# Decode layers on one core: split V load of head 5, two heads summed by columns, a last norm with both sums in one product

## The chip, the cores and the metric

The kernel runs on one core of a Trainium2 chip. The metric is the device time of one execution in microseconds (us). Three executions of the kernel before the change took 175.13, 175.47 and 176.53 us, median 175.47. One more execution was taken by the hardware profiler.

## What is computed

Four rows x of 512 elements (a batch of 4, one position each) go through attention, a gated MLP, the same attention and the same MLP, each with a residual. All inputs are bf16, and both layers of a kind use the same weights and the same caches. Cut to what matters:

```python
# x: (4, 1, 512); caches (4, 8, 8192, 128), the last W = 2048 positions are used; 32 query heads on 8 KV heads
def attn(x, k_cache, v_cache, wq, wo):
    q = (x @ wq)                                # 32 heads of 128
    p = softmax(q . k[:, :, Sk-W:] * 128**-0.5)
    return (p . v[:, :, Sk-W:]) @ wo            # 4096 -> 512
def mlp(x, w_gate, w_up, w_down):               # 512 -> 1792 -> 512
    return (sigmoid(x @ w_gate) * (x @ w_up)) @ w_down
x = x + attn(layernorm(x), ...); x = x + mlp(layernorm(x), ...)
x = x + attn(layernorm(x), ...); x = x + mlp(layernorm(x), ...)
```

## The kernel before

Everything is written as a list of named operations (`P.op`, with engine, estimated duration, and the tokens that it reads and writes). `_schedule` turns the list into one fixed order for each engine: it runs the list forward with the estimated durations and picks on each engine what can start first, and among what can start within 60 ns of that, the operation that stands earlier in the list. The order on the queue that issues DMAs (SP) is the order of the list. `_assign_sync` then adds the semaphore waits. Engines work their orders off strictly in turn, so an operation that waits holds all that stand behind it on its engine. `banks` adds waits where two engines use one PSUM bank.

The four layers are numbered 0 to 3. K of all 8 KV heads is loaded once, transposed and kept in `kt` as 256 units of 256 columns. V doesn't fit beside it: it is read for layer 0 and again for layer 2. In layer 2, V of heads 2 to 5 (`V2_2` to `V2_5`) is put over K of heads 0 to 3 as soon as these have given their scores, in one DMA of 2 MB each (L461, `load_v`); `V2_6` and `V2_7` come in pieces, and six units of head 7 are still there from layer 0. After them on the SP queue come the weights of the last MLP: `wg3_2`, `wu3_2` (the second halves of gate and up; the first halves are kept from layer 1) and four pieces of `w_down`, the last of them `wd3_12` (256 KB, to `side`).

One head of layer 2 goes: scores (L759), softmax (L768 to L792), probabilities spread to `pt` by DVE (L817) and ACT (L824), sums of the probabilities (`zb`, L832) and their reciprocal (L836). Then, two heads behind, the product with V. For heads 2 to 5 ("wide", L852) V is the moving operand, 32 matmuls of 256 columns; ACT copies the result out (L860) and four fp32 matmuls (L867) bring it back to columns. For heads 0, 1, 6 and 7 V is the stationary operand (L895), 64 matmuls. `omul` (L906) divides by the sum.

The product with wo has two forms. In the row form, heads 0 to 6 (`NWR = 7`), `sel` (L932, PE) and `osel` (L939, DVE) spread the head's columns, and four matmuls of 512 columns (L947) add it to row sums that stay in PSUM bank 7 over all heads. `early_residual` brings these sums back to columns once: `w_hi` (L960, ACT) copies bank 7 to bf16 and preloads the sigmoid table, `w_lo` (L966, DVE) takes the rest, `w_turn` (L973, PE) transposes both with 8 matmuls, `w_early` (L979, DVE) adds the result to x. In the column form, head 7 alone, 16 matmuls (L917) with wo as the stationary operand give columns that `xb_w_acc2_7` (L560) adds to x in bf16 (`xn`, what the last MLP multiplies) and `w_acc2_7` (L563) in fp32 (`xT`).

The last norm (`layer_norm(3)`) splits x into three bf16 parts (L583 to L586), sums them over the partitions in three matmuls (`ln_sum3`, L591), reduces (L597), subtracts the mean (L606), squares (L618), reduces (L621), sums over the partitions in an fp32 matmul (`ln_var3`, L579), and takes the power -1/2 on GpSimd (L630). The gate and up products (L1050, 8 pieces of 14 matmuls) don't wait for it: they use `xn` itself, and the mean and the scale are applied afterwards (L569 and the lines of L1066: `glu_gc`, `glu_gm`, then the sigmoid L1071, `glu_sr`, `glu_uc`, and `glu_h` L1090). `x_rows` (L1026) adds x, in rows, to the output's PSUM bank by 12 matmuls of 64 columns: three parts, two interleaved rows, two halves of the partitions. The w_down products (L1119, 56 matmuls) follow in the same bank, DVE copies the bank out (L1132), and one DMA writes the output.

## Time and profile before

| | |
|---|---|
| median of 3 executions | 175.47 us (175.13 to 176.53) |
| the profiled execution: its own time | 176.48 us |
| the profiled execution: span from first to last instruction | 174.6 us |
| mean granted TensorE clock | 0.792 of full speed |
| busy: PE, weight loads, DVE, ACT, GpSimd | 139.6, 102.3, 99.5, 75.4, 6.8 us |
| moved by DMA | 69.39 MB, mean 397 GB/s |
| L852 (PV of a wide head), 32 matmuls, at 140.96 us and at 152.99 us | 1.06 us and 1.88 us |
| L947 (wo, row form), 4 matmuls, at 150.00 us and at 160.51 us | 0.48 us and 0.60 us |
| L917 (wo, column form), 16 matmuls at 163.82 us | 0.59 us |
| L1026 (`x_rows`), 12 matmuls at 168.92 us | 1.44 us |
| L630 (power on GpSimd) at 167.99 us | 1.01 us |

The page cuts the span into 40 slices of 4.4 us, with each engine's busy share in tenths. PEclk is the clock that TensorE was granted, in tenths of full speed, and DMA is the mean busy share of the core's 16 DMA engines. The timeline names PE for matmuls and PEld for the weight loads before them. The chain of waits is followed back from the last instruction; a DMA in it starts where it was issued. "Landing" is when the data of a DMA have arrived and its semaphore says so.

### The profile page before, as it was taken

Reading aid. Unit: us, or ns where it says so; the run is one execution under the profiler, and the core shown is the slowest. Engines: PE = TensorE matmul, PEld = TensorE weight load, DVE = VectorE, ACT = ScalarE, POOL = GpSimd, SP = SyncE. Lnnn points to the kernel's source line nnn. Section 1 sums busy time; section 2 is a strip of 40 time slices with the busy share of each in tenths; the row PEclk is TensorE's granted clock in tenths of the full one; section 3 lists DMA queues with packets and bytes.
Section 4 is the critical chain, followed back from the end, with each engine's and each line's share of the span. In section 5 each row is a group of like instructions: output and inputs, shape, how many; then the busy total and the mean of one; then the engine's idle time right before and its main releaser. Section 6 shows DMA issues by size and latency. Waiting matters only on the chain.

```text
span 174.6 us, 4868 instructions
## 1 busy us (share of the span) xinstructions
PE 139.6 (80%) x2175; PEld 102.3 (59%) x2175; DVE 99.5 (57%) x246; ACT 75.4 (43%) x129; POOL 6.8 (4%) x17
## 2 busy tenths in 40 slices
PE   0395589899899679998969776548887999798794
PEld 0293488657566468564745466547424765576693
DVE  7435015886858484795897733014267988842440
ACT  2064216748476636566391240304424654730300
POOL 5200000000000000000000000100100000000020
PEclk9999755999999987999999755555555999955555
DMA  5999999999999999999999999999999999999940
GB/s 181 420 444 408 420 439 424 428 411 443 428 415 426 406 438 424 410 451 409 439 422 401 390 417 416 409 402 394 410 427 436 433 420 418 417 412 424 407 171 5
DMA packets 9504, 69.39 MB, mean 397 GB/s; under 512 B 1032, under 2 KB 2188, under 8 KB 6156
## 3 DMA queue, kind: packets, MB, share of 16 engines
q1 hardware_dynamic: 9476, 69.08, 95.3%
q8 instruction: 17, 0.28, 0.6%
q14 instruction: 3, 0.02, 0.0%
q10 hardware_dynamic: 8, 0.00, 0.0%
HBM read 69.08 MB, written 0.00 MB: 396 GB/s over the span
## 4 chain that ended last, share of the span: by engine, by line
DMA 54%; PE 33%; DVE 5%; ACT 4%; SPq 1%; issue 1%; DVEq 0%; ACTq 0%
DMA arena<-in_A_v_cache_dram 31%; DMA kt<-in_A_k_cache_dram 12%; PE ps L852 7%; PE ps L759 7%; DMA wo_sb<-in_B_w_gate_dram 6%; DMA wo_sb<-in_A_wq_dram 5%; PE ps L736 4%; PE ps L1050 3%; PE ps L895 3%; PE ps L867 2%; SPq L461 1%; PE ps L832 1%; PE ps L947 1%; ACT pb L781 1%; ACT pt L824 1%
## 5 line engine op out<-in xcount | busy, mean ns | idle before, releaser
L746 ACT COPY kt<-ps 128x1024 bf16<-128x1024 bf16 x40 | 39.3, 1016 | 28.9 <-PE ps L736 28.6
L736 PE MATMUL ps<-ident_r,kt 128*128 128x128 bf16 x512 | 40.6, 240 | 5.4 <-DMA kt<-in_A_k_cache_dram 3.2
L736 PEld LDWEIGHTS ps<-ident_r,kt 128*128 128x128 bf16 x512 | 35.3, 111 | 12.1 <-issue 4.0
L746 DVE COPY kt<-ps 128x1024 bf16<-128x1024 bf16 x24 | 29.1, 1214 | 15.1 <-PE ps L736 14.9
L759 PE MATMUL ps<-kt,qs 128*32 128x512 bf16 x256 | 20.4, 448 | 1.3 <-DVE qs L715 0.7
L817 DVE TENSOR_TENSOR pt<-ps,ofbr 128x1024 bf16<-128x1024 f32 (+1 forms) x15 | 15.4, 1030 | 2.7 <-PE ps L792 2.6
L852 PE MATMUL ps<-arena,pt 128*64 128x512 bf16 (+1 forms) x128 | 12.7, 361 | 3.1 <-DMA arena<-in_A_v_cache_dram 3.1
L768 DVE TENSOR_REDUCE nmz<-ps 128x1 f32<-128x512 f32 x16 | 11.0, 687 | 6.8 <-PE ps L759 6.5
L781 ACT ACTIVATE pb<-ps,nmz 128x512 bf16<-128x512 f32 x16 | 11.1, 695 | 5.7 <-DVE nmz L778 5.7
L787 DVE STREAM_TRANSPOSE pb<-pb 128x512 bf16<-128x512 bf16 x16 | 11.2, 702 | 3.8 <-ACT pb L781 3.8
L824 ACT ACTIVATE pt<-ps,ofbr 128x96 bf16<-128x96 f32 x28 | 7.2, 342 | 10.6 <-PE ps L792 10.6
L759 PEld LDWEIGHTS ps<-kt,qs 128*32 128x32 bf16 x256 | 5.9, 105 | 8.3 <-issue 2.6
L852 PEld LDWEIGHTS ps<-arena,pt 128*64 128x64 bf16 (+1 forms) x128 | 5.7, 106 | 7.9 <-DMA arena<-in_A_v_cache_dram 4.0
L832 PE MATMUL ps<-rowf,nmz 128*128 128x16 f32 x32 | 7.3, 304 | 2.3 <-DVE pt L817 2.2
L860 ACT COPY arena<-ps 128x512 f32<-128x512 f32 (+1 forms) x7 | 3.9, 555 | 11.6 <-PE ps L852 11.5
L832 PEld LDWEIGHTS ps<-rowf,nmz 128*128 128x128 f32 x32 | 5.7, 225 | 5.2 <-DVE pt L817 3.5
L630 POOL TENSOR_TENSOR rs<-pt,rs 128x4 f32<-128x4 f32 x4 | 4.1, 1013 | 119.8 <-DVE pt L626 119.8
L867 PEld LDWEIGHTS ps<-arena 128*128 128x128 f32 x52 | 6.7, 201 | 2.1 <-ACT arena L860 1.6
L867 PE MATMUL ps<-arena 128*128 128x16 f32 x52 | 7.4, 273 | 0.7
L1050 PE MATMUL ps<-xn,arena 128*128 128x5 bf16 (+1 forms) x168 | 6.3, 172 | 2.0 <-DMA arena<-in_B_w_up_dram 1.1
L1050 PEld LDWEIGHTS ps<-xn,arena 128*128 128x128 bf16 x168 | 6.3, 118 | 2.2 <-DMA arena<-in_B_w_up_dram 1.2
L947 PE MATMUL ps<-wo_sb,onr 128*16 128x512 bf16 x56 | 6.4, 442 | 1.4 <-DVE onr L939 1.4
(143 smaller groups left out, 158.0 us busy)
## 6 DMA issues: line engine op xcount, KB each, us to landing
kt<-in_A_k_cache_dram SPq DMA_DIRECT2D x8, 2048.0 KB, 24.8
arena<-in_A_v_cache_dram SPq DMA_DIRECT2D x7, 2048.0 KB, 20.1
kt<-in_A_v_cache_dram SPq DMA_DIRECT2D x4, 2048.0 KB, 15.6
wo_sb<-in_A_wo_dram SPq DMA_DIRECT2D x8, 512.0 KB, 25.4
kt<-in_A_v_cache_dram SPq DMA_DIRECT2D x3, 1024.0 KB, 17.0
kt<-in_A_wq_dram SPq DMA_DIRECT2D x1, 2048.0 KB, 11.8
side<-in_A_wq_dram SPq DMA_DIRECT2D x1, 1984.0 KB, 15.9
arena<-in_B_w_up_dram SPq DMA_DIRECT2D x2, 896.0 KB, 8.4
```

Of the source, the lines that this page charges most:

```text
L736: last = pe.transpose(bankb(bank)[:, (v * NB + q) * 128:(v * NB + q + 1) * 128], kt[:, c0:c0 + 128], ident_b[:, :])
L746: return (e.tensor_copy if ev == "vector" else e.copy)(to, fr)
L759: last = pe.matmul(ps[32 * b:32 * b + 32, sbk, 0:CB * 128], qs[:, q0:q0 + 32], blk_ap(kblk(h, b))[:, c * CB * 128:(c + 1) * CB * 128], sta ...
L768: lambda v: v.tensor_reduce(nmv, ps[:, sbk, 0:CB * 128], AXX, ALU.max, negate=True),
L781: o = a.activation(pbuf[:, :], ps[:, sbk, 0:CB * 128], ACTF.Exp, bias=gv, scale=1.0, accum_out=zv)
L787: P.op("vector", "ptr%d_%d" % (L, h), 650.0, lambda v: v.transpose(turned[:, :], pbuf[:, :]), r=[("pb", 0), ("pb", 1)], w=[("pb", 2), ("pb ...
L817: lambda v: v.tensor_tensor(pv4[:, 0:nj], spread(tbk, nj).unsqueeze(2).broadcast_to([128, nj, NB, REP]), ofb[:, :].unsqueeze(1).unsqueeze( ...
L824: last = a.mul(pv4[:, nj:NJ4, b, :], spread(MB, NJ4 - nj), ofb[:, b:b + 1])
L832: lambda pe: pe.matmul(ps[:, tbk, CB * NQ:CB * NQ + NR], zv.broadcast_to([128, 128]), rowf[:, :], start=True, stop=True),
L852: last = pe.matmul(ps[rows * g:rows * (g + 1), bank, 0:wide * 128].rearrange("p (c d) -> p c d", c=wide), ptv[:, w0:w0 + rows], v, start=( ...
L867: last = pe.matmul(ps[:, out[0], out[1]:out[1] + NR], part[:, c * 128:(c + 1) * 128], ey[wide][:, c * NR:(c + 1) * NR], start=(c == 0), st ...
L1050: last = pe.matmul(ps[:, bank, fc * wid:(fc + 1) * wid], cols[:, fc - g0, :], xn[:, ktc * (NB + 1):ktc * (NB + 1) + wid], start=(ktc == 0 ...
```

## The change

Five things change, all but the fourth in layers 2 and 3:

1. `V2_5` is loaded in two DMAs of 1 MB, one after the other on the SP queue in the place of the one, and `wide_pv` gives the product in two pieces of 16 matmuls, each with its own wait.
2. Head 6 leaves the row sums: `NWR` becomes 7 for layer 0 and 6 for layer 2. `early_residual(2)` stands ahead of head 6 in the list, with heads 0 to 5 in it. For head 6 `sel` and `osel` stay, a new reduction `oc` (DVE) drops the zeros of `osel`'s output, and `wo_cols` multiplies by wo in the column form, 16 matmuls into bank 5. Head 7's 16 matmuls add to the same columns.
3. The last norm: `s_keep` (GpSimd, in the norm of layer 2) keeps the sum of the old x; `early_shift` (DVE, behind `early_residual`) makes `xs` = x less its old mean. `last_norm` adds the new columns to `xs`, squares, reduces both in one instruction, and sums both over the partitions in one fp32 matmul. The variance comes from both sums in four small DVE instructions; the power stays on GpSimd. `ln_mean3` gives the mean that the gate and up corrections use.
4. The planner's estimate for a piece of the gate or up products is 36 ns per matmul in place of 29, in both MLPs.
5. `x_rows` takes 6 matmuls with a second identity of 64 columns (`eye64`, GpSimd). The three parts of x are put into the two halves of the partitions apart: two ACT copies each for the first and second part, two DVE subtractions for the third. After the sigmoid, `glu_sr` is gone, and `glu_ur` scales the up product (behind `glu_uc`) in its place.

```diff
-    NWR = 7
+    NWR = {0: HKV - 1, 2: HKV - 2}
...
+        sD = csum[:, HQ + 2 * NFC:HQ + 2 * NFC + NB]
...
+        lr1m, xs = tout[:, 0:NB], tin[:, 16:32]
...
+        xz, eye64 = qs[:, 0:168], qs[:, 168:232]
...
+        for h in range(2, HKV - 3):
             WHERE["V2_%d" % h] = [("kt", (h - 2) * UHEAD, UHEAD)]
+        WHERE["V2_%d" % (HKV - 3)] = [("kt", 3 * UHEAD, UHEAD // 2), ("kt", 3 * UHEAD + UHEAD // 2, UHEAD // 2)]
...
+                     (lr1m if L == 3 else lr1[:, :]).unsqueeze(1).broadcast_to([128, n, NB]),
...
+                P.op("gpsimd", "s_keep", 300.0, lambda g: g.tensor_copy(sD, lr1[:, :]), r=[("pss",)], w=[("sD",)])
...
+            for s, j0 in pieces:
+                qs_ = range(j0 // NJ, (j0 + s[2] * UNIT // 128) // NJ)
...
+                    for i, (tv, q, c) in enumerate(steps):
+                        if q not in qs_:
+                            continue
...
+                prev = [P.op("tensor", "PV%d_%d_%d" % (L, h, j0), (1800.0 if wide > 2 else 1060.0) / len(pieces), e_pv,
+                             r=blk_tok(s) + pk + (("pa", kp),), w=[("pvw", bank, j0)], banks=(bank,), order=prev)]
...
+                 r=toks, w=blk_tok((at[0], at[1], wide)), banks=(bank,))
...
+        XB, X0 = 5, 128
+        xsrc = ps[:, XB, X0:X0 + NX]
+        ocs = qs[:, 256:256 + NR]
...
+        def wo_cols(n, h, o_, tok):
+            def e_wo(pe):
...
+                for c in range(NC):
+                    for j in range(REP):
+                        last = pe.matmul(ps[:, XB, X0 + c * NB:X0 + (c + 1) * NB], dcol(wo_sb, c, h * WOH + j * D),
+                                         o_[:, j * NB:(j + 1) * NB], start=(n == NWR[2] and c == 0 and j == 0),
+                                         stop=(n == HKV - 1 and j == REP - 1), skip_group_check=True)
+                return last
+            P.op("tensor", "WO2_%d" % h, 600.0, e_wo, r=[("wo", h), tok], w=[("psl", XB, n)], banks=(XB,))
...
-            if n >= NWR:
+            if L and n == HKV - 1:
+                wo_cols(n, h, ov, ("on", k2))
+                return
...
-                residual("w_acc%d_%d" % (L, h), ps[:, obk, o0:o0 + NX], [("psl", obk)], obk, L == 2 and n == HKV - 1)
...
+            if L and n == NWR[2]:
+                def e_oc(v):
...
+                        return v.tensor_reduce(ocs.rearrange("p (j b) -> p j b", b=NB),
+                                               onr[:, :].rearrange("p (j r b) -> p j b r", r=REP, b=NB), AXX, ALU.add)
+                P.op("vector", "oc%d_%d" % (L, h), c_dve(4 * NR), e_oc, r=[("onr",), ("xz",)], w=[("oc",)])
+                wo_cols(n, h, ocs, ("oc",))
+                return
...
-                                     start=(n == 0), stop=(n == NWR - 1), skip_group_check=True)
+                                     start=(n == 0), stop=(n == NWR[L] - 1), skip_group_check=True)
...
+        def early_shift():
+            P.op("vector", "x_s", c_dve(NX),
+                 lambda v: v.scalar_tensor_tensor(
+                     xs.rearrange("p (c b) -> p c b", c=NC), sD.unsqueeze(1).broadcast_to([128, NC, NB]), -1.0 / D,
+                     xT[:, :].rearrange("p (c b) -> p c b", c=NC), ALU.mult, ALU.add),
+                 r=[("sD",), ("xT",)], w=[("tin",)])
...
+        def last_norm():
...
+            toks = [("psl", XB, n) for n in range(NWR[2], HKV)]
+            P.op("vector", "xb_last", c_dve(NX), lambda v: v.tensor_tensor(xnv, c4(xsrc), c4(xT[:, :]), ALU.add),
+                 r=toks + [("xT",)], w=[("xn",)], banks=(XB,))
+            P.op("vector", "ln_center3", c_dve(NX), lambda v: v.tensor_tensor(xc[:, :], xsrc, xs, ALU.add),
+                 r=toks + [("tin",)], w=[("xc",)], banks=(XB,))
+            P.op("vector", "ln_sq3", c_dve(NX), lambda v: v.tensor_tensor(sq[:, :], xc[:, :], xc[:, :], ALU.mult),
+                 r=[("xc",)], w=[("sq",)])
+            both = small[:, 768:896].bitcast(F32).rearrange("p (k y) -> p k y", k=2)[:, :, 0:NX].rearrange("p k (c b) -> p k b c", c=NC)
+            part = small[:, 976:1008].bitcast(F32).rearrange("p (k y) -> p k y", k=2)[:, :, 0:NB]
+            P.op("vector", "ln_r12_3", c_dve(2 * NX), lambda v: v.tensor_reduce(part, both, AXX, ALU.add),
+                 r=[("xc",), ("sq",)], w=[("lr2",)])
+            P.op("tensor", "ln_sum3", tm["pe_f32"],
+                 lambda t: t.matmul(ps[:, MB, 0:2 * NB].rearrange("p (k b) -> p k b", k=2), ones_f[:, 0:1].broadcast_to([128, 128]),
+                                    part, start=True, stop=True),
+                 r=[("lr2",), ("ones_f",)], w=[("psv",)], banks=(MB,))
+            s1, s2 = ps[:, MB, 0:NB], ps[:, MB, NB:2 * NB]
+            m2 = lr2[:, :]
+            P.op("vector", "ln_m1", c_dve(NB), lambda v: v.tensor_copy(lr1[:, :], s1), r=[("psv",)], w=[("lr1",)], banks=(MB,))
+            P.op("vector", "ln_m2", c_dve(NB), lambda v: v.scalar_tensor_tensor(m2, lr1[:, :], -1.0 / D, s1, ALU.mult, ALU.mult),
+                 r=[("psv",), ("lr1",)], w=[("lr2",)], banks=(MB,))
+            P.op("vector", "ln_v3", c_dve(NB), lambda v: v.tensor_tensor(m2, s2, m2, ALU.add),
+                 r=[("psv",), ("lr2",)], w=[("lr2",)], banks=(MB,))
+            P.op("vector", "ln_ve3", c_dve(NB),
+                 lambda v: v.tensor_scalar(lnl[:, :], m2, 0.0, D * EPS, ALU.max, ALU.add), r=[("lr2",)], w=[("lnl",)])
+            P.op("gpsimd", "ln_rstd3", 1000.0,
+                 lambda g: g.tensor_tensor(rstd[:, :], lnl[:, :], mhalf[:, :], ALU.pow),
+                 r=[("lnl",), ("mhalf",)], w=[("rstd",)])
+            P.op("vector", "ln_mean3", c_dve(NB), lambda v: v.tensor_tensor(lr1m, lr1[:, :], sD, ALU.add),
+                 r=[("lr1",), ("sD",)], w=[("tout",)])
+        def x_parts():
+            toks = [("psl", XB, n) for n in range(NWR[2], HKV)]
+            P.op("vector", "w_acc3", c_dve(NX), lambda v: v.tensor_tensor(xT[:, :], xsrc, xT[:, :], ALU.add),
+                 r=toks + [("xT",)], w=[("xT",)], banks=(XB,))
+            def by(a):
+                return a.rearrange("p (k i b) -> p k i b", k=2, i=2)
+            P.op("vector", "x_rest3", c_dve(NX), lambda v: v.tensor_tensor(by(xr), by(xT[:, :]), by2(xnv), ALU.subtract),
+                 r=[("xT",), ("xn",)], w=[("xr",)])
...
+            for hf in range(2):
+                o = slice(64 * hf, 64 * hf + 64)
+                P.op("scalar", "x_1_%d" % hf, c_act(NX), lambda a_, o=o, hf=hf: a_.copy(at(0, hf), by2(xnv)[o]),
+                     r=[("xn",), ("xz",)], w=[("x1", hf)])
+            for hf in range(2):
+                o = slice(64 * hf, 64 * hf + 64)
+                P.op("scalar", "x_2_%d" % hf, c_act(NX), lambda a_, o=o, hf=hf: a_.copy(at(1, hf), by(xr)[o]),
+                     r=[("xr",), ("xz",)], w=[("x2", hf)])
+            for hf in range(2):
+                o = slice(64 * hf, 64 * hf + 64)
+                P.op("vector", "x_3_%d" % hf, c_dve(NX), lambda v, o=o, hf=hf: v.tensor_tensor(at(2, hf), by(xr)[o], at(1, hf), ALU.subtract),
+                     r=[("xr",), ("x2", hf), ("xz",)], w=[("x3", hf)])
...
         def x_rows():
-            P.op("gpsimd", "x_1", 300.0, lambda g: g.tensor_copy(x_at[3][0], by2(xnv)), r=[("xn",), ("xz",)], w=[("x1",)])
...
-                last = None
...
-                            a0 = 32 * (1 - half) + 2 * part + i
-                            last = pe.matmul(ps[:, YB, i:128:2], xz[:, a0:a0 + 128], ident_b[:, 64 * half:64 * half + 64],
-                                             start=(part + i + half == 0), stop=False, skip_group_check=True)
+                for y in range(6):
+                    last = pe.matmul(ps[:, YB, y % 2:128:2], xz[:, 32 + y:160 + y], eye64, start=(y == 0), stop=False,
+                                     skip_group_check=True)
...
-            P.op("tensor", "x_rows", 12 * tm["pe_pair"], e_x, r=[("x1",), ("x2",), ("x3",), ("ident_b",)],
+            P.op("tensor", "x_rows", 700.0, e_x, r=[("x%d" % a, hf) for a in (1, 2, 3) for hf in range(2)] + [("eye64",)],
...
-            layer_norm(L)
+            if last_layer:
+                last_norm()
+                x_parts()
+            else:
+                layer_norm(L)
...
-                prev = [P.op("tensor", "glu_%s%d_%d" % (nm, L, ktc), tm["pe_pair"] * NFC, e_g,
+                prev = [P.op("tensor", "glu_%s%d_%d" % (nm, L, ktc), 36.0 * NFC, e_g,
...
-                mul("glu_gm", gm, fb(tg), rs3, [mg, ("rstd",)], ("gm",))
+                root = float(D) ** 0.5
+                P.op("vector", "glu_gm%d" % L, c_dve(NH_),
+                     lambda v: v.scalar_tensor_tensor(fb(gm), fb(tg), root, rs3, ALU.mult, ALU.mult), r=[mg, ("rstd",)], w=[("gm",)])
                 P.op("scalar", "glu_sig%d" % L, c_act(NH_), e_sig, r=[("gm",)], w=[("sg",)])
-                mul("glu_sr", sg, fb(sg), rs3, [("sg",), ("rstd",)], ("sg",))
                 mul("glu_uc", um, fb(pu), fb(tu), toks["u"] + [mu], ("um",), (UB,), ALU.subtract)
+                P.op("vector", "glu_ur%d" % L, c_dve(NH_),
+                     lambda v: v.scalar_tensor_tensor(fb(um), fb(um), root, rs3, ALU.mult, ALU.mult),
+                     r=[("um",), ("rstd",)], w=[("um",)])
...
-            if n == NWR:
+            if n == NWR[2]:
                 early_residual(2)
+                early_shift()
...
+        P.op("gpsimd", "eye64", 300.0, lambda g: g.tensor_tensor(eye64, ident_b[:, 0:64], ident_b[:, 64:128], ALU.add),
+             r=[("ident_b",), ("xz",)], w=[("eye64",)])
```

More of the change, by code (lines that the diff above doesn't have):

```diff
@@ L445, in build @@
         })
-        for h in range(2, HKV - 2):
+        for h in range(2, HKV - 3):
             WHERE["V2_%d" % h] = [("kt", (h - 2) * UHEAD, UHEAD)]
+        WHERE["V2_%d" % (HKV - 3)] = [("kt", 3 * UHEAD, UHEAD // 2), ("kt", 3 * UHEAD + UHEAD // 2, UHEAD // 2)]
         def bankb(b):
@@ L837, in weights, with wide_pv @@
                  r=[("psz", tbk)], w=[("rz", kp)], banks=(tbk,))
-        def wide_pv(L, n, h, wide, bank, out, s):
+        def wide_pv(L, n, h, wide, bank, out, pieces):
             kp, ptv, pk = pt_of(L, n)
@@ L880, in pv_wo @@
             if wide:
-                assert len(pieces) == 1
-                wide_pv(L, n, h, wide, obk if L else 5, (obk, p0), pieces[0][0])
+                wide_pv(L, n, h, wide, obk if L else 5, (obk, p0), pieces)
                 pieces = [(None, 0)]
@@ L942, in pv_wo @@
                  r=[("psl", obk), ("ofr",)], w=[("onr",)], banks=(obk,))
+            if L and n == NWR[2]:
+                def e_oc(v):
+                    with nc.allow_low_precision("three of four are zero"):
+                        return v.tensor_reduce(ocs.rearrange("p (j b) -> p j b", b=NB),
[3 more added lines that the diff above has]
+                return
             def e_wo(pe):
@@ L957, in early_residual @@
             hi, lo = pb[:, 0:D], pb[:, D:2 * D]
-            tk = [("psw", n) for n in range(NWR)]
+            tk = [("psw", n) for n in range(NWR[L])]
             def e_hi(a):
```

45 lines of the change are left out of this document (24 added, 21 removed).

## The prediction

> **What bounds the kernel now.** I read the slices of the page first, then the chain of waits from its end backwards, then the landing of each DMA of the last stage, then windows of 3.41 us for the clock. The slices:
>
> ```profile
> PEclk9999755999999987999999755555555999955555
> DMA  5999999999999999999999999999999999999940
> ```
>
> The DMA engines are full from 4 us to 166 us. So up to there only the bytes count, and the change adds none. What can be won lies behind: the span ends at 174.6 us. The chain of waits there:
>
> ```profile
> 158.11 0.53 PE ps L947 x2
> 158.64 0.98 PE ps L895 x32
> ...
> 160.51 0.64 PE ps L947 x4
> 161.15 0.02 issue
> 161.17 0.59 ACT pb L960
> 161.76 0.02 issue
> 161.79 0.70 DVE pb L966
> 162.49 0.14 issue
> 162.62 0.35 PE ps L973 x8
> 162.98 0.57 PE ps L895 x20
> ...
> 163.82 0.60 PE ps L917 x16
> ...
> 169.06 1.31 PE ps L1026 x12
> 170.37 0.09 issue
> 170.46 1.71 PE ps L1119 x56
> ```
>
> No DMA is in it: from 152.8 us on PE's own queue sets the end, with short waits for DVE and ACT. The transfers are not far behind, as the issues of V of head 5, of the last piece of V of head 7 and of the last w_down show (KB, us from issue to landing):
>
> ```profile
> kt<-in_A_v_cache_dram SPq DMA_DIRECT2D x1, 2048.0 KB, 17.9
> ...
> kt<-in_A_v_cache_dram SPq DMA_DIRECT2D x1, 640.0 KB, 17.2
> ...
> side<-in_B_w_down_dram SPq DMA_DIRECT2D x1, 256.0 KB, 20.1
> ```
>
> They were issued at 134.43, 144.23 and 149.92 us, so they landed at 152.3, 161.4 and 170.0. In the same way the halves of V of head 6 landed at 154.8 and 157.4 and the first piece of head 7 at 159.8. PE took them at 152.99, 162.98 (head 7's last), 171.69 (w_down), 156.21, 158.58 and 161.05: 0.7 to 1.7 us after the landing. That distance is all that a shorter chain can win.
>
> Third, the clock, in windows whose edges I put on its own steps (columns: length, PE, weight loads, DVE, ACT, GpSimd busy, granted clock, DMA):
>
> ```profile
> 149.65:153.07 3.42, 2.63 (x35) 1.88 (x39) 2.93 (x10) 2.66 (x9) 0.00 (x0) 0.99 0.99 417
> 153.07:156.48 3.41, 3.27 (x53) 2.30 (x46) 1.67 (x4) 1.38 (x6) 0.00 (x0) 0.50 1.02 417
> ```
>
> The clock fell to 0.50 at 153.03 and never rose again. In the window before, PE was busy 2.63 us of 3.42. At 0.50 the 32 matmuls of L852 take 1.88 us in place of 1.06.
>
> **The change part by part**, against the profiled execution (176.48 us: span 174.6 and 1.88 around it).
>
> *V of head 5 in halves.* The bytes are the same. The two 1 MB halves of head 6 landed 5.1 us apart from head 5's landing (152.3 to 157.4), the 2 MB transfers 4.9 us apart (142.6, 147.5, 152.3). So halves cost 0.24 us, and all later landings move by that; one more issue on SP (0.54 us by its row) is hidden, since the next one, at 137.80, waits for scores. The first half is there at about 150.0. PE is idle for 3.42 − 2.63 = 0.79 us in 149.65 to 153.07, and half of L852 at full clock is 0.53, so it fits into idle time. If that is all, the path gets 0.53 us shorter. If PE is also faster there, 1.2 (L852 done at 153.7 in place of 154.9). I take 0.5. Cover gone: if the first half isn't there when PE's queue gets to it, head 4's sums and wo stand behind it.
>
> *Row sums without head 6.* Now PE's queue holds head 7's last 20 matmuls behind `w_turn`, which waits for `w_hi` and `w_lo`: from the end of the 32 matmuls before it (162.08, at 161.05 plus 1.03) to 162.62 is 0.54 us of idle PE, and then 0.35 us for `w_turn` itself. With the sums closed by head 5's L947 (end 158.64), `w_hi` (0.59), `w_lo` (0.70) and the hand-overs (0.18) end at 160.1, and `w_turn` runs while PE waits for head 6's L906 and L939 anyway (0.28 and 0.30 us idle there). I count 0.54 + 0.28 = 0.82 gained, 0.07 of `w_turn` staying on the path. Head 6's wo: 4 matmuls of 512 columns (0.60) become 16 narrow ones (L917: 0.59), so nothing. `oc` stands between `osel` and these: 0.22 by L939 plus 0.03, 0.25 us, with PE idle and head 7's matmuls queued behind. Adding head 7 to the same columns costs nothing: the same 16 matmuls. `early_shift` (0.17 by L606) has DVE idle around it. Sum: 0.82 − 0.25 = 0.57.
>
> Both together would bring head 7's last matmuls forward by 1.07. The landing allows 162.98 − 161.43 − 0.24 − 0.05 = 1.26. So 1.07 stands, close to its floor.
>
> *From the end of head 7's wo (164.42) to the first w_down matmul (170.46)*: 6.04 us now, on a chain that ends with GpSimd's power (169.0), L1066, sigmoid, L1066, `glu_h` at 170.20 and `x_rows`, whose 12 matmuls end at 170.37. After: DVE's sum for `xn` and hand-over 0.26; 112 gate and up matmuls at 1.07/28 = 0.038 are 4.29; one fp32 product 0.43 (L579); the three of L591 are gone. PE is through at 4.98. Then `glu_uc` 0.21, `glu_ur` 0.22, `glu_h` 0.26, gaps and hand-overs 0.13: 5.80. `glu_ur` is new behind the last up product, `glu_sr` was not. `x_rows` is 6 x 0.109 = 0.65 behind the up products and ends at 5.63, hidden. The norm: four DVE steps of 0.21 to the reduced sums (0.85), the fp32 product behind 28 products (1.33 to 1.76), four steps (2.6), power 1.01 and hand-over (3.7). The gate product is ready at 0.26 + 84 x 0.038 + 0.43 = 3.9. So the power comes off the path with 0.2 us to spare, and the two subtractions of `x_parts` (0.23 each) would cost at most 0.3 if DVE takes them first. Gain 6.04 − 5.80 = 0.24; I take 0.2. The four ACT copies (0.25 each by L1071's row) lie ahead of the sigmoid, 2 us earlier. `s_keep` and `eye64` (0.27 by L1018) find GpSimd idle; the first is done before the power of layer 2 is asked for, as that comes four DVE steps later.
>
> *The planner's 36 ns* moves no product past another that I can see: in layer 1 the pieces wait for DMAs. From −0.2 to +0.2, taken as 0.
>
> The 56 w_down matmuls would then start at 169.2 and end at 170.9. The last piece lands at 170.0 + 0.24 and needs 0.45, so the floor is 170.7. Sum: 0.5 + 0.57 + 0.2 = 1.27 us. 176.48 − 1.27 = 175.2; against the median, 175.47 − 1.27 = 174.2. The bounds of the parts, with the floor, are 0.9 and 1.45: 174.0 to 174.6.
>
> **The rivals.**
>
> *The clock stays up.* The window to 153.07 would get 0.53 us of matmuls: about 3.1 of 3.42. Of the earlier windows at full clock those with 2.68 and more kept it, as did one with 2.59 and one with 2.28; those with 2.63, 2.41 and 2.07 lost it. If it stays, the rest of head 5 (L852, and L867: 1.03 against 0.62) is through 1 us sooner, but head 6's halves land at 155.0 and 157.7, and the narrow matmuls gain little (L895 28.6 ns each at full clock, 32 at half). So it gives the floor, 1.45 us: 174.0. The Trainium skill, "TensorE: Matmul & The Clock Gate", "What's actually happening", has the clock fall after an idle window of about 3.4 us. The steps at 136.00 and 153.07 are five such windows apart, but the trace has no idle window before the fall, only one busy to 77%, so busy time decides here. Chance 0.2.
>
> *The transfers end it anyway.* The median run is 1.0 us faster than the profiled one. If its chain is that much shorter and its transfers are the same, the end is the floor: 170.0 + 0.24 + 0.45 + 0.34 for DVE's copy + 2.12 for the output = 173.2, plus 1.88 = 175.05. Gain 0.4: 174.9 to 175.3. The Trainium skill, "DMA: Bandwidth & Descriptors", "Measured", lists 341 GB/s for 1 MB and 425 for 16 MB; by that, as an estimate, head 5 would land 1.3 us later, which would take the gain as well. The halves of head 6 came at 397 to 425 GB/s, so this trace disagrees. Chance 0.2.
>
> *`w_turn` in the wrong place, slower.* It now waits for ACT and DVE with more of PE's work behind it. If PE's order has it ahead of the second half of head 6 (taken at 158.58), PE idles until 160.1, and head 6 and 7 stand behind: 1.47 idle and 0.35 for itself, less 0.89 that the old place cost, plus 0.25 for `oc` and 0.24 for the halves, less 0.2: 1.2 us; 0.7 with the gain from head 5. 175.9 to 176.7, and up to 177.4 if the first half of head 5 also holds PE. It decides from the point where `w_lo` ends later than the second half of head 6 lands (157.7). For it: `w_lo` would end near 159.5. Against: the order goes by what can start first, and that half can. Chance 0.2.
>
> **How the numbers follow.** My forecast has 0.4: 174.2, its own range 174.0 to 174.6. A difference of 1% (1.75 us) is about what can be told from none. The floor, 1.45 us, lies below that, so faster by over 1% needs transfers that end earlier as well: 0.08 out of the first two cases. Slower by over 1% (above 177.2) is the end of the third: 0.08. Within 1%: 0.84. From 173.6, for a transfer end 0.4 us earlier, to 176.3, half way into the third case, leaves out 0.2.
>
> **What would show it.** Right: in the timeline L852 in two groups of 16, the first before 152 us; L973 ahead of head 6's L932 and no longer followed by head 7's 20 matmuls; head 7's column product ending near 163.4; L630 ending well before the last gate product; `x_rows` ending before `glu_h`; the first w_down matmul near 169.2. Wrong: L973 with idle PE ahead of head 6's matmuls, a first half of head 5 that PE waits for, a DMA at the end of the chain, landings more than 0.3 us later, or a power that still ends last.

## The result and the profile after

| | before | after |
|---|---|---|
| median of 13 executions each, one chip | 175.92 us (174.92 to 176.79) | 174.82 us (174.55 to 175.06) |
| the profiled execution: own time, span | 176.48, 174.6 us | 174.91, 173.2 us |
| its mean granted TensorE clock | 0.792 | 0.819 |

The ratio is 0.9938, with a 95% interval from 0.9915 to 0.996: 1.1 us faster, within 1% of before. The after times also lie closer together: 0.5 us from the shortest to the longest, 1.9 us before. All medians and ranges below leave out executions that took over 1.5% longer than the fastest of the same kernel: four of 90 later ones of the kernel before, two of one other run.

The slices of the page of the kernel after (granted clock and DMA share, in tenths, 40 slices of 4.33 us):

```profile
PEclk9999656999999999999999655555576999985555
DMA  5999999999999999999999999999999999999970
```

The clock still falls in the last stage, at 154.9 us (1.00 of full before it, 0.50 behind it), and doesn't come back. The DMA engines are full for as long as before. The end of the chain of waits of the kernel after (start, us, engine, output, line; L922 is head 6's and 7's product with V, L896 `wo_cols`, L1152 gate and up, L1225 w_down; in this and the chains below, steps between the lines are left out):

```profile
143.17 18.37 DMA kt<-in_A_v_cache_dram
161.58 0.73 PE ps L922 x20
162.59 0.60 PE ps L896 x16
163.45 1.07 PE ps L1152 x28
164.95 2.73 PE ps L1152 x84
168.68 1.57 PE ps L1225 x48
```

Before, no DMA stood in this stretch. Now the last piece of V of head 7 does: issued at 143.17, landed at 161.54, taken at 161.58. Head 5's product, `w_hi`, `w_lo`, `w_turn` and `x_rows` are all gone from the chain. The DMA issues of the kernel after, the groups of V's halves, head 7's last piece and the last piece of w_down (KB, median us from issue to landing):

```profile
kt<-in_A_v_cache_dram SPq DMA_DIRECT2D x5, 1024.0 KB, 18.5
...
kt<-in_A_v_cache_dram SPq DMA_DIRECT2D x1, 640.0 KB, 18.4
...
side<-in_B_w_down_dram SPq DMA_DIRECT2D x1, 256.0 KB, 20.4
```

The halves of head 5 landed at 150.03 and 152.51 (before, the whole at 152.33); head 6's at 155.14 and 157.52; head 7's last piece at 161.57 (161.37); the last w_down at 170.21 (170.02). These are sums of issue and time to landing, good to some 0.05 us; the chain has 161.54 where the sum gives 161.57. In this pair of executions everything behind the halves comes 0.2 us later. That need not be the halves' doing: from head 4's landing to the end of head 5's it is 4.9 to 5.0 us in three traces in which head 5 comes whole (5.0 in one of before), and 4.9 to 5.1 in four in which it comes in halves (5.1 in this one). So the halves cost between nothing and 0.2 us. PE's timeline in the last stage of the kernel after (start, us, shapes, in brackets the idle time just ahead and who ended it):

```profile
150.10 0.62 PE L864 MATMUL ps<-kt,pt 128*32 128x256 bf16 x16 [0.47 <-DMA kt<-in_A_v_cache_dram]
...
152.58 0.62 PE L864 MATMUL ps<-kt,pt 128*32 128x256 bf16 x16 [0.21 <-DMA kt<-in_A_v_cache_dram]
...
155.21 1.04 PE L922 MATMUL ps<-pt,kt 128*128 128x32 bf16 x32 [0.33 <-DMA kt<-in_A_v_cache_dram]
...
157.55 1.03 PE L922 MATMUL ps<-pt,kt 128*128 128x32 bf16 x32
158.43 0.35 PE L1011 MATMUL ps<-rqb,pb 128*128 128x4 bf16 x8
...
159.82 0.59 PE L896 MATMUL ps<-qs,wo_sb 128*128 128x4 bf16 x16 [0.64 <-DVE qs L976]
...
161.58 0.72 PE L922 MATMUL ps<-kt 128*128 128x32 bf16 x20 [0.30 <-DMA kt<-in_A_v_cache_dram]
...
167.53 0.80 PE L1124 MATMUL ps<-qs 128*128 128x64 bf16 x6
168.68 0.61 PE L1225 MATMUL ps<-arena,pt 128*25 128x128 bf16 x16 [0.35 <-DVE pt L1196]
...
170.26 0.40 PE L1225 MATMUL ps<-side,pt 128*25 128x128 bf16 x8
```

PE now takes V where it lands, and mostly waits for it: 0.47 and 0.21 us for the two halves of head 5 (L864), 0.33 for the first half of head 6, 0.30 for head 7's last piece; head 6's second half is taken at 157.55 (landed 157.52). `w_turn` (L1011) runs right behind head 6's 32 matmuls with no idle time. `x_rows` (L1124) is done before `glu_h` (L1196) lets w_down begin. The last w_down matmuls start at 170.26, 0.05 us behind their landing. At both ends of this stretch it is a transfer that PE waits for.

### The profile page after: what moved, and what is told of

The parts are those of the page before. It is cut to its first block, busy times and chain, and to the rows that moved or that the text cites. A ratio compares the mean times of both kernels' runs of the same rounds, so it can differ in the third digit from the quotient of the medians.

```text
span 173.2 us, 4888 instructions
## 1 busy us (share of the span) xinstructions
PE 135.6 (78%) x2178; PEld 98.5 (57%) x2178; DVE 100.0 (58%) x251; ACT 76.4 (44%) x133; POOL 7.0 (4%) x18
## 4 chain that ended last, share of the span: by engine, by line
DMA 57%; PE 28%; DVE 6%; ACT 5%; issue 1%; SPq 1%; DVEq 0%; ACTq 0%
DMA arena<-in_A_v_cache_dram 32%; DMA kt<-in_A_v_cache_dram 11%; DMA arena<-in_A_wq_dram 10%; PE ps L764 5%; PE ps L864 5%; DMA wo_sb<-in_A_wq_dram 4%; PE ps L1152 4%; PE ps L741 4%; PE ps L673 2%; PE ps L922 2%; ACT pb L786 1%; ACT pt L829 1%; ACT wo_sb L1028 1%; PE ps L1225 1%; SPq L464 1%
## 5 line engine op out<-in xcount | busy, mean ns | idle before, releaser
L741 PE MATMUL ps<-ident_r,kt 128*128 128x128 bf16 x512 | 38.6, 232 | 4.9 <-DMA kt<-in_A_k_cache_dram 2.7
L741 PEld LDWEIGHTS ps<-ident_r,kt 128*128 128x128 bf16 x512 | 33.1, 106 | 11.7 <-issue 4.4
L764 PE MATMUL ps<-kt,qs 128*32 128x512 bf16 x256 | 19.3, 426 | 1.7 <-ACT pb L786 1.0
L864 PE MATMUL ps<-arena,pt 128*64 128x512 bf16 (+1 forms) x128 | 13.4, 391 | 4.6 <-DMA arena<-in_A_v_cache_dram 4.6
L864 PEld LDWEIGHTS ps<-arena,pt 128*64 128x64 bf16 (+1 forms) x128 | 6.0, 117 | 10.1 <-DMA arena<-in_A_v_cache_dram 6.0
L837 PE MATMUL ps<-rowf,nmz 128*128 128x16 f32 x32 | 6.7, 285 | 2.8 <-DVE pt L822 2.6
L837 PEld LDWEIGHTS ps<-rowf,nmz 128*128 128x128 f32 x32 | 5.2, 203 | 5.8 <-DVE pt L822 4.1
L1152 PE MATMUL ps<-xn,arena 128*128 128x5 bf16 (+1 forms) x168 | 6.2, 172 | 2.0 <-DMA arena<-in_B_w_up_dram 1.1
L1152 PEld LDWEIGHTS ps<-xn,arena 128*128 128x128 bf16 x168 | 6.2, 118 | 2.2 <-DMA arena<-in_B_w_up_dram 1.2
L1028 ACT COPY wo_sb<-ps 128x1024 bf16<-128x1024 bf16 x4 | 4.0, 1012 | 7.6 <-DMA wo_sb<-in_A_wq_dram 7.5
L635 POOL TENSOR_TENSOR rs<-pt,rs 128x4 f32<-128x4 f32 x3 | 3.0, 1015 | 107.0 <-DVE pt L631 107.0
```

What stands on the lines that cost most here:

```text
L741: last = pe.transpose(bankb(bank)[:, (v * NB + q) * 128:(v * NB + q + 1) * 128], kt[:, c0:c0 + 128], ident_b[:, :])
L764: last = pe.matmul(ps[32 * b:32 * b + 32, sbk, 0:CB * 128], qs[:, q0:q0 + 32], blk_ap(kblk(h, b))[:, c * CB * 128:(c + 1) * CB * 128], sta ...
L837: lambda pe: pe.matmul(ps[:, tbk, CB * NQ:CB * NQ + NR], zv.broadcast_to([128, 128]), rowf[:, :], start=True, stop=True),
L864: last = pe.matmul(ps[rows * g:rows * (g + 1), bank, 0:wide * 128].rearrange("p (c d) -> p c d", c=wide), ptv[:, w0:w0 + rows], v, start=( ...
L1152: last = pe.matmul(ps[:, bank, fc * wid:(fc + 1) * wid], cols[:, fc - g0, :], xn[:, ktc * (NB + 1):ktc * (NB + 1) + wid], start=(ktc == 0 ...
```

## The experiments

The question: is the 1.1 us what the three parts took off the chain, as in the prediction, or do the transfers end both kernels, and the change only closes a distance that differs from run to run? In all kernels but one, told below, the time stands about 1.75 us above the span, so spans are compared too.

**One part undone or done alone.** V of head 5 whole again, in the kernel after:

```diff
-        for h in range(2, HKV - 3):
+        for h in range(2, HKV - 2):
             WHERE["V2_%d" % h] = [("kt", (h - 2) * UHEAD, UHEAD)]
-        WHERE["V2_%d" % (HKV - 3)] = [("kt", 3 * UHEAD, UHEAD // 2), ("kt", 3 * UHEAD + UHEAD // 2, UHEAD // 2)]
```

> The changed kernel with V of head 5 loaded and multiplied whole again. Theory A (each part takes its own term off PE's path): the halves were worth about 0.5 us, so of the gain of 1.1 us 0.3 to 0.7 is lost: ratio to the kernel before 0.996 to 0.998, and PE takes the first half of V of head 6 more than 0.5 us after its landing. Theory B (in the changed kernel the landings alone set the end, so there is slack on PE): less than 0.2 us is lost, and since the later landings come 0.2 us earlier without the halves it may even gain: ratio 0.992 to 0.995.

Head 6 back in the row sums, in the kernel after:

```diff
-    NWR = {0: HKV - 1, 2: HKV - 2}
+    NWR = {0: HKV - 1, 2: HKV - 1}
```

> The changed kernel with head 6 back in the row sums (the early residual stands ahead of head 7 again); the last norm and the six products stay. Theory A: the part was worth 0.57 us, so 0.4 to 0.7 us is lost, ratio 0.996 to 0.998, with about 0.5 us of idle PE ahead of the transposes of the row sums and head 7's last products behind them. Theory B: under 0.2 us lost, ratio 0.993 to 0.995.

The last norm, `x_rows` in 12 matmuls and `glu_sr` as before, in the kernel after:

```diff
...
-            if last_layer:
-                last_norm()
-                x_parts()
-            else:
-                layer_norm(L)
+            if last_layer:
+                residual("w_acc2_7", xsrc, [("psl", XB, n) for n in range(NWR[2], HKV)], XB, True)
+            layer_norm(L)
...
```

> The changed kernel with the old last norm (three parts summed, then the centred squares), twelve products for the rows of x and the old scaling after the sigmoid; the halves and the column sums of heads 6 and 7 stay. Theory A: the norm part was worth 0.2 us: ratio 0.994 to 0.996. Theory B (the end is the landing of the last weights, 0.3 to 0.4 us of which the w_down products wait for): 0 to 0.1 us lost, ratio 0.993 to 0.9945. Theory C (once the products come earlier, the power on GpSimd is what is late): 0.4 us or more lost, ratio above 0.9965, with the first w_down product 0.5 us or more later than in the changed kernel counted from the end of head 7's column product.

The halves of head 5 alone, in the kernel before:

```diff
-        for h in range(2, HKV - 2):
+        for h in range(2, HKV - 3):
             WHERE["V2_%d" % h] = [("kt", (h - 2) * UHEAD, UHEAD)]
+        WHERE["V2_%d" % (HKV - 3)] = [("kt", 3 * UHEAD, UHEAD // 2), ("kt", 3 * UHEAD + UHEAD // 2, UHEAD // 2)]
...
-                wide_pv(L, n, h, wide, obk if L else 5, (obk, p0), pieces[0][0])
+                wide_pv(L, n, h, wide, obk if L else 5, (obk, p0), pieces)
```

> The kernel before with V of head 5 in halves and nothing else. Theory A: PE's path is 0.5 us shorter up to head 7: ratio 0.996 to 0.998. Theory B (the wait for the row sums ahead of head 7's last products, or another one, takes the gain back): within 0.2 us, ratio 0.999 to 1.001.

The kernel after, unchanged, in another series:

> The changed kernel itself, on the same chip as the three beside it. In the 13 executions so far its span lies between 172.8 and 173.2 us at granted clocks of 0.801 to 0.838, while the 35 spans of the kernel before lie between 172.8 and 175.6 and are longer the lower the clock. Theory A (the changed kernel's end is set by the transfers whatever the clock; the kernel before reaches that only with a high clock): again a spread of at most 0.6 us, no longer span at a low clock, median 1.0 to 1.5 us below the median of before. Theory B (the narrow spread was that chip's or that hour's): a spread above 1.2 us, longer at a low clock.

| | time, median (us) | span, median (least to most) | ratio to before |
|---|---|---|---|
| before, beside the first four | 175.83 | 174.1 (172.8 to 175.4) | |
| after, head 5 whole | 175.57 | 173.8 (172.7 to 174.9) | 0.9981 [0.9944, 1.0019] |
| after, head 6 in rows | 175.62 | 173.2 (172.7 to 173.8) | 0.9981 [0.9947, 1.0016] |
| after, old norm and `x_rows` | 175.21 | 173.5 (173.1 to 174.0) | 0.9972 [0.9938, 1.0005] |
| before, halves alone | 175.29 | 173.5 (172.9 to 174.5) | 0.9989 [0.9958, 1.0021] |
| before, beside the next | 175.96 | 174.2 (173.0 to 175.6) | |
| after again | 174.80 | 173.05 (172.7 to 173.7) | 0.9942 [0.9915, 0.9969] |

The first five rows come from one chip, the last two from another. The whole gain comes back there (1.2 us). Each part undone loses some of it, but against before all four single intervals hold 1, and after again stands on another chip, so the sizes here are medians with a few tenths of doubt. By these, the halves are worth 0.8 us (175.57 − 174.80) where they are taken away and 0.5 where they are put in alone (0.2 by the ratio, 0.9989); the norm with `x_rows` 0.4; head 6's columns 0.15 us of span. The spread of after again, 1.0 us of span, is wider than the first time (0.4) and lies between what its two readings expected.

The chain of waits of the kernel after with head 5 whole shows what the halves do (L863 is head 5's product, L997 and L1003 `w_hi` and `w_lo`, L921 narrow products with V):

```profile
152.04 0.74 DVE pt L821
153.59 1.73 PE ps L863 x32
159.12 0.59 ACT pb L997
159.74 0.69 DVE pb L1003
162.46 1.42 PE ps L921 x52
```

This run's mean clock was 0.803. PE waits for DVE (L821, probabilities), and then all 32 matmuls of head 5 lie behind that and take 1.73 us. All that follows is late: PE gets to head 7's 52 matmuls at 162.46 and takes them in one go, with both pieces landed (the last at 161.2). With the halves, 16 of the 32 are done before DVE is waited for (they start at 150.10 in the kernel after). Four executions of this kernel had a mean clock of 0.828 or more and spans of 172.7 to 173.0 us, like the kernel after; the other eight, at 0.811 or less, took 173.7 to 174.9. So here, what the halves are worth shows at a low clock alone.

In the kernel with the old norm `x_rows` was in the chain again (L1129, 12 matmuls; L1224 is w_down):

```profile
168.07 1.30 PE ps L1129 x12
169.47 1.85 PE ps L1224 x51
```

so w_down began at 169.47 in place of 168.68. The power on GpSimd isn't in that chain.

**The clock.** The hardware doesn't grant each execution the same clock. The runs of before (86, in three series) and of after (25, in two) by their mean granted clock:

| mean granted clock | before: runs, median span (least to most) | after: runs, median span (least to most) |
|---|---|---|
| below 0.800 | 11, 174.9 (174.0 to 175.4) | 4, 173.05 (172.7 to 173.3) |
| 0.800 to 0.814 | 32, 174.5 (173.9 to 175.6) | 7, 173.0 (172.8 to 173.7) |
| 0.815 to 0.829 | 20, 173.7 (173.0 to 174.9) | 10, 172.9 (172.8 to 173.4) |
| 0.830 and above | 23, 173.3 (172.8 to 173.9) | 4, 173.15 (173.1 to 173.2) |

Before's median span grows by 1.6 us from the highest clock to the lowest; after's doesn't move. Both have the same shortest span, 172.7 to 172.8. So there is a floor that doesn't go with the clock, and the change takes off what stood above it: nearly 2 us where the clock was low, as in the profiled execution of before, and next to nothing where it was high.

**Is the floor the transfers?** In the profiled execution of after again (clock 0.795, span 173.1) no DMA stands in the chain from 120 us on: PE takes head 7's 52 matmuls in one go from 160.71 to 162.28, with the last piece landed at about 161.5. But the last w_down matmuls start at 170.17, 0.05 us behind their landing, as in the first one. So PE's queue and the transfers end close together in the kernel after. To part them, the second piece of V of head 1 is loaded in layer 2 with 256 of its 2816 columns (640 KB less; that head's product then uses old contents in their place), in the kernel after and in the kernel before:

```diff
-                dma("V%d_%d_%d" % (L, h, u0), blk_ap(s), v_d[h][:, :, u0 * UNIT:(u0 + n) * UNIT], w=blk_tok(s),
+                m = 1 if L == 2 and h == 1 and u0 else n
+                dma("V%d_%d_%d" % (L, h, u0), blk_ap(s)[:, 0:m * UNIT], v_d[h][:, :, u0 * UNIT:(u0 + m) * UNIT], w=blk_tok(s),
```

> The changed kernel with 640 KB less to transfer: of the second piece of V of head 1 in layer 2 only the first 256 of 2816 columns are loaded, the rest of that piece is multiplied as it lies there. Nothing else differs, the order on every engine is the same, and all later landings come about 1.6 us earlier. Theory A (its end is set by the transfers): the median is 0.8 to 1.6 us below the changed kernel's, until PE's chain is the bound, and the spread over clocks comes back. Theory B (PE's chain sets the end): less than 0.4 us.

> The kernel before with the same 640 KB less to transfer, of V of head 1 in layer 2. Theory A (its end is set by PE's chain in most executions): the median moves by 0.5 us at most, the lowest spans by 0.5 to 1.5, and the spread over clocks grows beyond 2.8 us. Theory B (transfers set the end of the kernel before as well): all spans 1.2 us shorter or more.

After with fewer bytes: 174.39 us, span 172.6 (171.7 to 173.1), ratio to before 0.989 [0.9856, 0.9924]. That is 0.4 us below after by the medians and 0.9 by the ratios, while 640 KB take 1.6 us at the 417 GB/s of the windows; in its trace the last landings are 1.1 us earlier than in the kernel after (160.4 and 169.1). Its spans tend to go with the clock again: from 171.7 at 0.839 to 173.1 at 0.804. Before with fewer bytes: 174.80, span 173.0 (172.0 to 174.4), ratio 0.9944 [0.9908, 0.9979], 1.2 us below before by the medians and 1.0 by the ratio. Neither reading of the second run held: before isn't held by PE's queue alone, since earlier V helps it, and not by the transfers alone, since the spread with the clock stays. In the kernel after the floor gives way, by 0.4 to 0.9 us, so the transfers do set it; then PE's own chain comes next. In the trace of the kernel after with fewer bytes the last of that chain reads (L1153 gate and up, L1226 w_down):

```profile
161.47 0.60 PE ps L897 x16
162.33 1.07 PE ps L1153 x28
163.83 2.72 PE ps L1153 x84
168.06 1.05 issue
169.11 1.47 PE ps L1226 x45
```

Head 7's wo is 1.1 us earlier than in the kernel after and so is the end of the gate and up products; then PE stands for 1.05 us within the w_down products, with 11 of them done, and the profile shows nothing that it waits for. It took back what the earlier V had brought in this execution. The next run has more such pauses.

**`w_turn` in the wrong place.** `w_turn` ordered ahead of head 6's second half, in the kernel after:

```diff
...
-                             ..., w=[("pso", obk, j0)], banks=(obk,), order=prev)]
+                             ..., w=[("pso", obk, j0)], banks=(obk,),
+                             order=list(prev) + ([turn_op[2]] if L and n == 6 and j0 else []))]
...
+            turn_op[L] = P.op("tensor", "w_turn%d" % L, 8 * tm["pe_pair"], e_turn,
```

> The changed kernel with one change of PE's order: the 8 matmuls that turn the row sums stand ahead of the 32 of the second half of head 6 in place of behind them. This is the slower rival of the prediction by itself. From the trace of the changed kernel: the sums close at 156.78, the two copies end at 158.16, so the half of head 6 starts at 158.55 in place of 157.55. Rival right: about 0.8 us slower than the changed kernel, as head 7's last products then start 0.8 us after their landing. If there is slack behind: under 0.2 us.

175.80 us, span 174.05 (173.7 to 174.5), ratio to before 1.0003 [0.9983, 1.0022]: 1.0 us lost, all of the gain. Its chain of waits (L1007 `w_lo`, L1014 `w_turn`, L922 head 6 and then head 7, L896 `wo_cols`):

```profile
157.25 0.56 DVE pb L1007
157.94 0.35 PE ps L1014 x8
158.30 0.89 PE ps L922 x32
160.40 0.59 PE ps L896 x16
160.99 1.42 PE ps L922 x52
162.69 0.60 PE ps L896 x16
163.84 0.26 issue
169.70 0.29 issue
```

PE waits 0.67 us for `w_lo`, and by its timeline takes head 6's second half at 158.16, 0.6 us behind where the kernel after takes it (157.55). But head 7's wo ends at 163.29, only 0.1 us behind the kernel after (163.19): there the landing of head 7's last piece (161.5 in both) covers most of the delay. The other 0.7 us by which the w_down products end later (171.47 against 170.69) arise behind that, with two pauses of PE, 0.26 us in the gate and up products and 0.29 us behind the 11th w_down matmul. So the order loses the gain in all 12 executions (its shortest span is after's longest, 173.7), but the trace doesn't show the wait for `w_lo` as the reason.

The timelines of all twelve traces have four such pauses of PE from 140 us on: these two, the 1.05 us of the kernel after with fewer bytes, also behind the 11th w_down matmul, and 0.25 us at 149.52 in the kernel before. All end 2.4 to 2.5 us behind the start of a transfer on the DMA queue that the page lists as "instruction" (161.65, 167.60, 166.65 and 147.25 us; 17 of them in an execution, 0.28 MB in all). PE that waits for its own instructions would look like that. It is not shown: no run moved these transfers, and the profile doesn't say which engine they are for.

**More work on PE, to raise the clock.** The row product with wo twice for heads 2, 3 and 4, in the kernel before (the sums then hold these heads twice):

```diff
-                for j in range(4):
+                for j in list(range(4)) * (2 if L and 2 <= n <= 4 else 1):
```

> The kernel before, in which PE gives the row product with wo (L947) twice for heads 2, 3 and 4 of layer 2: 4 more matmuls of 512 columns each, so the products of these heads are added twice to the sums. Theory A, the clock spreads the kernel before: PE's own queue sets its end, and how fast it is there depends on how much of the last 45 us PE gets at the full clock. More work in stretches in which PE otherwise waits for V makes its windows of 3.41 us fuller, so the clock is raised earlier or kept longer: a mean granted clock above before's by 0.01 or more, and a time no longer than before's, possibly shorter (174.9 to 176.0 us, against before's 176.0). Theory B, the clock only goes along with the time and PE's work is what counts: the work of the last of the three, 0.48 us at full and 0.60 us at half clock, less what of it lies in the idle time ahead of the landing of head 5 (0.8 us), so 0 to 0.6 us more: 176.0 to 176.6, with the same clock. Both give the same where the clock does not rise; what tells them apart is time against clock over the runs.

175.69 us beside 175.41 for before in the same series, ratio 1.0018 [0.9977, 1.0058]; the mean clock over the runs was 0.822 and 0.823. The clock was not raised, so this run doesn't decide whether a raised clock would shorten before. The table above shows that time goes with the clock; that the clock makes it was not shown by changing it. Windows of the profiled execution (length, then PE, weight loads, DVE, ACT, GpSimd busy, granted clock, DMA):

```profile
149.65:153.07 3.42, 2.65 (x42) 1.84 (x34) 3.02 (x10) 2.62 (x10) 0.00 (x0) 0.98 1.00 414
153.07:156.48 3.41, 3.26 (x44) 1.66 (x45) 1.19 (x3) 0.96 (x5) 0.00 (x0) 0.52 1.01 417
156.48:159.90 3.42, 3.20 (x90) 2.83 (x90) 1.41 (x5) 0.77 (x4) 0.00 (x0) 1.00 1.02 420
```

Here the clock came back at 156.5 us, which it had not done in the profiled execution of before, and the span, with the added products in it, was no shorter (174.7 against 174.6).

**Head 6 in the row sums, again:**

> The kernel after, with head 6 back in the row sums, a second time and in more rounds. The first time its spans were 172.7 to 173.8 us with a median of 173.2, only 0.2 us above the kernel after's, but the times stood 2.4 to 2.8 us above the span in 8 of 12 runs, where every other kernel stands 1.75 above. Theory A, the part is worth 0.57 us as predicted: spans with a median of 173.6, times 175.4, always 1.75 apart. Theory B, the part is worth 0.2 us, since the landing of head 7's last piece hides most of it, and the distance was chance: spans at 173.2, times at 175.0. Theory C, the distance belongs to this kernel: it comes back, and the time is 175.6 with spans at 173.2.

175.18 us beside 175.41 for before, ratio 0.9999 [0.9971, 1.0028]; span 173.05 (172.6 to 173.7), the same as after's. The distance of time and span came back: above 1.9 us in 8 of 12 runs both times (2.0 to 2.8), while no other kernel's run reaches it. The chain of this kernel (L998 `w_hi`, L1004 `w_lo`, L1011 `w_turn`):

```profile
159.51 0.59 ACT pb L998
160.13 0.70 DVE pb L1004
160.96 0.35 PE ps L1011 x8
161.32 0.57 PE ps L922 x20
```

The wait for `w_lo` stands ahead of head 7's last 20 matmuls again, and yet they start at 161.32, no later than in the kernel after (161.58). The piece had landed earlier here, at 161.0, so the wait costs some 0.3 us at this place; at the end PE takes the last w_down at 169.68, 0.1 us behind its landing, so a transfer hides that again. So the columns take nothing off the span; of the 0.4 to 0.8 us of time that their absence costs (175.18 and 175.62 against 174.80, on different chips), nearly all lies outside the span, and what it is there stays open.

## Why the prediction came out

The forecast was 174.2 us, in a range of 173.6 to 176.3; measured 174.82. Its gain, 1.27 us, was 1.10 and 1.16 in the two series. The level was 0.6 too low: the bounds that the prediction worked out from its parts, 174.0 to 174.6, don't hold the result; the wider range, opened for the rivals, does. That the sum of the gain came near is in part luck: the second of its three terms was too large, and the first (by the run without it) and the third were too small.

- **The step that failed** is "against the median, 175.47 − 1.27 = 174.2". The gain was worked out in an execution with a low clock (0.792, own time 176.48) and then taken off a median of others. The prediction's own end by the transfers, 173.2 us of span, is what the profiled execution of after had (173.2), and the other executions of after lie within 0.5 us of it. What is above it differs from one to the next, so the gain does, too: 1.57 us between the two profiled ones, next to none between runs of a high clock. The median to go out from was low as well: 175.47 in three runs, 175.92 in thirteen.
- **Halves of head 5**: mechanism right in the main (two groups, the first taken at 150.10). PE did wait for the first half, 0.47 us with other work behind it; the second half, for which it waits as well, covers that. The price of 0.24 us for later landings rests on a landing of head 6's second half at 157.4; its issue at 138.38 and 18.9 us to landing give 157.3, and a price of 0.07. The traces give 0 to 0.2. The term was 0.5, the runs give 0.8 taken away and 0.2 to 0.5 put in alone. It had been priced between 0.53 at full and 1.2 with a faster PE; the lower end was taken.
- **Row sums without head 6**: the marks held. `w_turn` moved ahead of head 6's `sel` and cost PE no wait, `oc` took 0.22 us, head 7's wo ended at 163.2 (163.4 said). But the term, 0.57 us, is 0 to 0.15 of span. It was added to the halves' 0.5 as if PE stayed late; once the halves have brought PE forward, the landings cover the wait for `w_lo`. The check against the floor (1.07 of 1.26) couldn't show this, since it was made for the one late execution.
- **From head 7's wo to w_down**: 5.80 us said, 5.50 measured (163.18 to 168.68), 0.2 said for the gain, 0.5 measured between the two traces (6.04 before) and 0.4 by the run without it. The size of the gate and up products was off: 0.038 us each from the first group of 28 was put on all 112, but the other 84 took 2.73 us in the chain above, 0.0325 each. The `x_rows` products are hidden, as said. The power was to end 0.2 us ahead of the gate product; the timelines of DVE and GpSimd have the power from 165.93 to 166.95 and the gate product ready at 166.8 for `glu_gc`, whose end at 167.00 is 0.05 us behind the power. It sets nothing, with almost nothing to spare.
- **The planner's 36 ns**: taken as 0. With 29 ns in its place every engine's order and that of the DMA queue come out the same, so this part does nothing.
- **Rival, the clock stays up**: it fell (at 154.9 us), and the time was near the floor all the same. In the 3.45 us ahead of the fall PE was busy for 2.39, not the 3.1 of 3.42 that the rival counted on. Nor does busy time alone decide, as the prediction has it: in the kernel before, the windows with 2.28 us and, left out there, 2.42 (from 13.12 us) kept the clock, and the one with 2.63 lost it. What the rival missed is that after's span doesn't go with the clock. By the Trainium skill, "TensorE: Matmul & The Clock Gate", "What's actually happening", an idle window of about 3.4 us takes the clock away; the windows above have it fall at 153.07 behind one in which PE was busy for 2.65 of 3.42 us, so the trace doesn't agree, if idle means without work.
- **Rival, the transfers end it anyway**: right on what ends the kernel after (in the first trace a landing is in the chain, PE waits 0.30 us for it), and its 174.9 us is nearest to the measured 174.82. Wrong on the gain, 0.4: over thirteen runs before's median is 0.6 us faster than its profiled execution, not 1.0. The estimate by the Trainium skill's "DMA: Bandwidth & Descriptors", "Measured", 1.3 us later for two transfers of 1 MB, isn't borne out: in the full queue here the second half landed 0.2 us later than the whole.
- **Rival, `w_turn` in the wrong place**: it didn't come. Put there by hand it cost 1.0 us over after and nothing over before, where the rival had 0.7 to 1.2 over before. PE waited as described, but the trace has only 0.1 us of that left at the end of head 7's wo; the rest comes with pauses whose cause is open. The rival put the end of `w_lo` near 159.5; it came at 158.16 (157.81 in that run), since with the halves the row sums close earlier.
- **The marks of a wrong prediction**: two of them came, a first half of head 5 that PE waits for (0.47 us) and a DMA at the end of the chain.

## What to carry to other kernels

A change that shortens one engine's queue where transfers stand a little behind it is worth, in each execution, only what that execution is above the transfers' end; so work out that end first, as a time, and don't take a gain found in one profiled execution off the median of others. Where two parts shorten the same queue, price the second one with the first in place. Look at the granted clock over many runs: if the time of a kernel goes with it, the kernel may have an engine on its path that the transfers could hide.

## What the runs showed of the hardware

The same program gets a mean granted clock between 0.790 and 0.852 from run to run, and the span of the kernel before, whose end hangs on PE, goes with it over 2.8 us (172.8 to 175.6); the spans of the kernel after lie within 1.0 (172.7 to 173.7) and don't. Wide matmuls suffer most (32 of 256 columns: 1.06 and 1.88 us), narrow ones little (32 columns: 24 in 0.60 us at full clock, from 135.02 in the chain of after, and 20 in 0.57 us at half, from 162.98 in that of before). PE stood for up to 1.05 us with nothing shown that it waited for, each time until 2.4 to 2.5 us behind the start of a transfer on the instruction queue. And with head 6 in the row sums the time stands 2.0 to 2.8 us above the span in 16 of 24 runs, where all other kernels stand at 1.7 to 1.9; what it is stays open.
